# A spectral-mixing and gated-MLP kernel: separate PSUM banks for the inverse transform and the MLP sums, the MLP one pass behind, a fourth bank for its first product and six staging buffers

## The chip, the cores and the metric

The kernel runs on one core of a Trainium2 chip. The metric is the device time of one execution in microseconds. A ratio is the mean time of one kernel's runs over the mean of the other's in the same rounds, so it is not quite the ratio of the medians quoted beside it.

## The reference

```python
batch, seq, dim = 8, 3008, 256          # x: (8, 3008, 256) float32
X = np.fft.rfft(x, axis=1)
y = np.fft.irfft(X * (filt_r + 1j*filt_i)[None], n=seq, axis=1)
t = y.reshape(24064, 256)
h = t @ w_in                            # 256 -> 2048
g = h * (1 / (1 + np.exp(-beta * h)))
out = g @ w_out                         # 2048 -> 256
```

## The kernel before

The first half (to about 618 us) makes cosine and sine tables and does the forward transform and the filter, and passes its result through DRAM. The second half works in 24 passes: three column blocks (512, 512 and 481 columns) of eight batches. Because the transform is real, one pass gives two blocks of tokens, "lo" and "hi". The first product of the MLP is called hps, its sigmoid sig, its gated value gT; the code and the prediction call the MLP "MoE". PSUM, to which TensorE writes its products, is used in banks of 128x512 float32; copying a sum from there to a staging buffer (ostage) is called an eviction.

```python
tc.tile_pool(name="inv_psum", bufs=1, space=PSUM) as ipsum,     # ps0..ps3: four banks
tc.tile_pool(name="moe_psum", bufs=3, space=PSUM) as mpsum,     # hps: three banks
...
for bb in range(B):
    ps = [ipsum.tile([P, 512], F32, tag=f"ps{q}") for q in range(4)]
    psA, psB = ps[0:2], ps[2:4]
    # 24 matmuls with cos into psA; ACT copies psA -> a_sb; 24 with sin into psB
    # DVE: yT_lo = a_sb + psB ; yT_hi = reversed(a_sb - psB)           (4 operations)
    for yT, tbase, jmin, jmax in (lo, hi):
        for fb in range(16):
            hps = mpsum.tile([P, 512], F32, tag="hps")
            # 2 matmuls: hps = w_in[:, fb].T @ yT
            nc.scalar.activation(sig, hps, ACT.Sigmoid, scale=beta)
            nc.vector.tensor_tensor(gT, hps, sig, ALU.mult)
            for tb in range(4):                          # sums in the SAME four banks ps[tb]
                nc.tensor.matmul(ps[tb][:, :256], lhsT=gT[:, tb], rhs=wout_sb[:, fb], ...)
        for tb in range(4):
            ost = mpool.tile([P, 256], F32, tag="ostage")    # three buffers
            nc.scalar.activation(ost, ps[tb][:, :256], ACT.Copy)
            nc.sync.dma_start(out[...], ost[...])
# ... (cut)
```

The program is written in a framework whose scheduler fixes the order of each engine's instructions when the kernel is built. The order therefore stays fixed on the chip.

Of the kernel before, what the change touches and what calls it, by code (L numbers as in the profile page):

```python
# [10 lines left out]
P = 128  # L11

ACT = mybir.ActivationFunctionType
ALU = mybir.AluOpType
F32 = mybir.dt.float32
BF16 = mybir.dt.bfloat16
# [5 lines left out]
def _cdiv(a, b):  # L22
    return (a + b - 1) // b


def _rev_free(ap: AP, count: int) -> AP:
    assert len(ap.shape) == 2 and ap.shape[1] >= count
    base_step = ap.ap[1][0]
    return AP(ap.tensor, ap.offset + (count - 1) * base_step, [ap.ap[0], [-base_step, count]])
# [3 lines left out]
def kernel(  # L33
# [10 lines left out]
    nc = tc.nc  # L44

    B, S, D = x.shape
# [17 lines left out]
    NDC = D // P  # L64
    NFB = FF // P
# [27 lines left out]
    beta_sb = consts.tile([P, NFB], F32, name="beta_sb", tag="beta_sb")  # L93
# [13 lines left out]
    with (  # L107
# [54 lines left out]
        for mm in range(NMH):  # L162
            m0 = mm * P
            pm = min(P, HB - m0)
            j0 = 1 if mm == 0 else 0
            j1 = pm - 1 if (m0 + pm - 1 == KSP) else pm
# [28 lines left out]
        for kb in range(NKB):  # L195
# [5 lines left out]
            for cb in range(NCBF):  # L201
                c0 = cb * CB
                xr_ps = fpsum.tile([P, CB], F32, name="xr_ps", tag="xr_ps")
                xi_ps = fpsum.tile([P, CB], F32, name="xi_ps", tag="xi_ps")
                for mm in range(NMH):
# [4 lines left out]
                        lhsT=cos_tab[:pm, mm, :Kb],  # L210
                        rhs=xe_sb[:pm, mm, c0 : c0 + CB],
                        start=(mm == 0),
                        stop=(mm == NMH - 1),
                    )
                for mm in range(NMH):
# [4 lines left out]
                        lhsT=sin_tab[:pm, mm, :Kb],  # L220
                        rhs=xo_sb[:pm, mm, c0 : c0 + CB],
                        start=(mm == 0),
                        stop=(mm == NMH - 1),
# [43 lines left out]
    with (  # L267
# [3 lines left out]
        tc.tile_pool(name="inv_misc", bufs=2) as imisc,  # L271
        tc.tile_pool(name="moe_sb", bufs=3) as mpool,
        tc.tile_pool(name="inv_psum", bufs=1, space=bass.MemoryType.PSUM) as ipsum,
        tc.tile_pool(name="moe_psum", bufs=3, space=bass.MemoryType.PSUM) as mpsum,
    ):
        def load_inv_tables(icb):
            n0i = icb * 512
            cols = min(512, NMH * P - n0i)
            ct = itab.tile([P, NKB, 512], BF16, name="cos_ti", tag="cos_ti")
            st = itab.tile([P, NKB, 512], BF16, name="sin_ti", tag="sin_ti")  # L280
            nc.sync.dma_start(ct[:, :, :cols], tcos_dram[icb * P : (icb + 1) * P, :, :cols])
            nc.scalar.dma_start(st[:, :, :cols], tsin_dram[icb * P : (icb + 1) * P, :, :cols])
            return ct, st
# [31 lines left out]
        win_sb = wpool.tile([P, NDC, FF], BF16, name="win_sb", tag="win_sb")  # L315
        wout_sb = wpool.tile([P, NFB, D], BF16, name="wout_sb", tag="wout_sb")
        with tc.tile_pool(name="wstage", bufs=1) as wstage:
# [5 lines left out]
            for fb0 in range(0, NFB, WOB):  # L323
# [7 lines left out]
                )  # L331
                nc.vector.tensor_copy(wout_sb[:, fb0 : fb0 + nfb, :], wout_st[:, :nfb, :])

        for ncb in range(NNI):
            n0 = ncb * 512
            Nn = min(512, HB - n0)
            cos_ti, sin_ti = tabs_cur
            if ncb + 1 < NNI:
                tabs_cur = load_inv_tables(ncb + 1)

            hi_jmin = 1 if (n0 <= KSP < n0 + Nn) else 0
            hi_jmax = Nn - 1 if n0 == 0 else Nn

            for bb in range(B):
                ps = []
                for q in range(2 * NDC):
                    pt = ipsum.tile([P, 512], F32, name=f"ps{q}", tag=f"ps{q}")
                    ps.append(pt)
                psA = ps[0:NDC]
                psB = ps[NDC : 2 * NDC]  # L350
                for kk in range(NKB):
                    Kk = min(P, NF - kk * P)
                    for dc in range(NDC):
                        col0 = bb * D + dc * P
                        nc.tensor.matmul(  # L355
                            psA[dc][:, :Nn],
                            lhsT=yr_grps[kk // KKG][:Kk, kk % KKG, col0 : col0 + P],
                            rhs=cos_ti[:Kk, kk, :Nn],
                            start=(kk == 0),
                            stop=(kk == NKB - 1),  # L360
                        )
                a_sb = []
                for dc in range(NDC):
                    at = imisc.tile([P, 512], F32, name=f"a_sb{dc}", tag=f"a_sb{dc}")
                    nc.scalar.activation(at[:, :Nn], psA[dc][:, :Nn], ACT.Copy)  # L365
                    a_sb.append(at)
                for kk in range(NKB):
                    Kk = min(P, NF - kk * P)
                    for dc in range(NDC):
                        col0 = bb * D + dc * P  # L370
                        nc.tensor.matmul(  # L371
                            psB[dc][:, :Nn],
                            lhsT=yi_grps[kk // KKG][:Kk, kk % KKG, col0 : col0 + P],
                            rhs=sin_ti[:Kk, kk, :Nn],
                            start=(kk == 0),
                            stop=(kk == NKB - 1),
                        )
                yT_lo = imisc.tile([P, NDC, 512], BF16, name="yT_lo", tag="yT_lo")
                yT_hi = imisc.tile([P, NDC, 512], BF16, name="yT_hi", tag="yT_hi")
                for dc in range(NDC):  # L380
                    nc.vector.tensor_tensor(  # L381
                        yT_lo[:, dc, :Nn], a_sb[dc][:, :Nn], psB[dc][:, :Nn], ALU.add
                    )
                for dc in range(NDC):
                    nc.vector.tensor_tensor(
                        yT_hi[:, dc, :Nn],
                        _rev_free(a_sb[dc][:, :Nn], Nn),
                        _rev_free(psB[dc][:, :Nn], Nn),
                        ALU.subtract,
                    )  # L390

                nchunk = _cdiv(Nn, P)
                blocks = [
                    (yT_lo, bb * S + n0, 0, Nn),
                    (yT_hi, bb * S + (S - n0 - Nn + 1), hi_jmin, hi_jmax),
                ]
                for yT, tbase, jmin, jmax in blocks:
                    for fb in range(NFB):
                        hps = mpsum.tile([P, 512], F32, name="hps", tag="hps")
                        for dc in range(NDC):  # L400
                            nc.tensor.matmul(  # L401
                                hps[:, :Nn],
                                lhsT=win_sb[:, dc, fb * P : (fb + 1) * P],
                                rhs=yT[:, dc, :Nn],
                                start=(dc == 0),
                                stop=(dc == NDC - 1),
                            )
                        sig = mpool.tile([P, 512], F32, name="sig", tag="sig")
                        nc.scalar.activation(  # L409
                            sig[:, :Nn],  # L410
                            hps[:, :Nn],
                            ACT.Sigmoid,
                            scale=beta_sb[:, fb : fb + 1],
                        )
                        gT = mpool.tile([P, 512], BF16, name="gT", tag="gT")
                        nc.vector.tensor_tensor(gT[:, :Nn], hps[:, :Nn], sig[:, :Nn], ALU.mult)  # L416
                        for tb in range(nchunk):
                            tw = min(P, Nn - tb * P)
                            nc.tensor.matmul(  # L419
                                ps[tb][:tw, :D],  # L420
                                lhsT=gT[:, tb * P : tb * P + tw],
                                rhs=wout_sb[:, fb, :],
                                start=(fb == 0),
                                stop=(fb == NFB - 1),
                            )
                    for tb in range(nchunk):
                        tw = min(P, Nn - tb * P)
                        j0 = max(tb * P, jmin)
                        j1 = min(tb * P + tw, jmax)
                        if j1 <= j0:  # L430
                            continue
                        ost = mpool.tile([P, D], F32, name="ostage", tag="ostage")
                        nc.scalar.activation(ost[:tw], ps[tb][:tw, :D], ACT.Copy)  # L433
                        nc.sync.dma_start(
                            out[tbase + j0 : tbase + j1, :],
                            ost[j0 - tb * P : j1 - tb * P],
                        )


# [28 lines left out]
```

## Time and profile before

| | before |
|---|---|
| time, median (lowest to highest) | 1737.94 us (1735.37 to 1740.11), 12 runs |
| first MLP matmul starts | 618.0 us |
| period of a 512-column pass | 45.74 us, of which TensorE needs 38.3 |
| period of a 481-column pass | 47.85 us, of which TensorE needs 36.8 |
| start of the last evictions to the end of the span | 14.8 us |

The rows of the timeline below read: start, duration, engine and line, operation, output and inputs, shape, count, and in brackets the idle time ahead and who ended it. PE is TensorE (PEld its weight loads), ACT is ScalarE, DVE is VectorE. These are lines of the kernel before that the prediction does not show. First, the shares of the engines in the chain of work that ended last.

```profile
PE 48%; DVE 17%; DMA 15%; ACT 10%; SPq 4%; issue 4%; another core or an unknown queue 2%; ACTq 0%; DVEq 0%
```

```profile
1719.46 0.94 ACT L433 ACTIVATE ostage<-ps 128x256 f32<-128x256 f32 x3 [1.07 <-PE ps L419]
...
1727.17 0.38 ACT L433 ACTIVATE ostage<-ps 97x256 f32<-97x256 f32 x1 [6.78 <-DMA out_dram<-ostage]
```

At the very end the fourth eviction waits 6.78 us for a staging buffer. The view of busy time by stretch shows one pass: its columns are length, busy time (and count) of each engine, granted TensorE clock (1.00 is full speed), DMA share and GB/s.

```profile
core 0: us, PE busy (x) PEld busy (x) DVE busy (x) ACT busy (x) POOL busy (x), PEclk, DMA share, GB/s
...
653.39:699.13 45.74, 41.17 (x236) 21.52 (x241) 23.64 (x36) 24.40 (x43) 0.00 (x0) 1.00 0.07 24
```

TensorE is shown busy 41.2 of 45.7 us, ACT and DVE only half of it.

### The profile page before, as it was taken

The numbers are of one execution on the slowest core, as the hardware profiler recorded it, in microseconds if no ns is written. First come the engines' busy times: TensorE is split into PE (matmuls) and PEld (weight loads), VectorE is DVE, ScalarE is ACT, GpSimd is POOL, SyncE is SP. The second block draws the span as 40 slices with busy tenths as digits, with TensorE's granted clock in tenths as the row PEclk, the third lists the DMA queues.
The fourth block names the chain that finished last, engine by engine and source line by source line (L and its number), as shares of the span: only waits on it lengthen the run. The fifth ranks groups of instructions, "written<-read, shape, count | busy, mean of one in ns | idle before, by whom it ended". The sixth has DMA issues, their size and how long they took to land.

```text
span 1734.2 us, 18868 instructions
## 1 busy us (share of the span) xinstructions
PE 1302.2 (75%) x7100; PEld 665.6 (38%) x7200; DVE 926.4 (53%) x1332; ACT 681.0 (39%) x1322; POOL 4.2 (0%) x19
## 2 busy tenths in 40 slices
PE   0032259999980278898988888999888988888886
PEld 0010024444440034444444444444444544444443
DVE  6044469999980054555554555554555544444444
ACT  1000103333210055555555555555555554444444
POOL 0000000000000000000000000000000000000000
PEclk9965579999995689999999999999999999999998
DMA  4178312212257200000002000000000000000000
GB/s 148 60 248 295 126 55 97 95 70 86 88 193 296 93 22 25 25 25 23 18 22 98 25 25 25 25 25 25 25 25 25 15 21 23 22 14 23 23 24 23
DMA packets 89058, 113.64 MB, mean 66 GB/s; under 512 B 7497, under 2 KB 81923, under 8 KB 87943
## 3 DMA queue, kind: packets, MB, share of 16 engines
q1 hardware_dynamic: 56757, 67.39, 11.6%
q10 hardware_dynamic: 32209, 45.05, 7.5%
q8 instruction: 56, 0.92, 0.2%
q14 instruction: 36, 0.29, 0.1%
HBM read 66.00 MB, written 58.72 MB: 72 GB/s over the span
## 4 chain that ended last, share of the span: by engine, by line
PE 48%; DVE 17%; DMA 15%; ACT 10%; SPq 4%; issue 4%; another core or an unknown queue 2%; ACTq 0%; DVEq 0%
PE ps L419 17%; PE hps L401 11%; DVE gT L416 8%; ACT sig L409 7%; PE ps L371 7%; DMA xb<-xrev_dram 6%; PE ps L355 5%; PE xr_ps L208 4%; DMA out_dram<-ostage 3%; PE xi_ps L218 3%; SPq L169 3%; DMA yr_dram<-yr_stage 2%; ACT ostage L433 2%; DMA yrg<-yr_dram 2%
## 5 line engine op out<-in xcount | busy, mean ns | idle before, releaser
L409 ACT ACTIVATE sig<-hps,beta_sb 128x512 f32<-128x512 f32 (+1 forms) x768 | 498.3, 680 | 383.1 <-PE hps L401 382.8
L416 DVE TENSOR_TENSOR gT<-hps,sig 128x512 bf16<-128x512 f32 (+1 forms) x768 | 500.4, 678 | 263.0 <-ACT sig L409 233.5
L419 PE MATMUL ps<-wout_sb,gT 128*128 128x256 bf16 (+1 forms) x3072 | 470.3, 274 | 85.3 <-DVE gT L416 80.6
L419 PEld LDWEIGHTS <-gT 128*128 128x128 bf16 (+1 forms) x3072 | 262.2, 100 | 357.6 <-DVE gT L416 309.4
L208 PE MATMUL xr_ps<-xe_sb,cos_tab 128*128 128x512 bf16 (+2 forms) x563 | 153.3, 406 | 160.8 <-DVE xe_sb L189 157.5
L381 DVE TENSOR_TENSOR yT_lo<-a_sb,ps 128x512 bf16<-128x512 f32 (+1 forms) x48 | 30.3, 674 | 376.6 <-PE ps L371 376.6
L401 PE MATMUL hps<-yT_lo,win_sb 128*128 128x512 bf16 (+1 forms) x741 | 217.0, 376 | 16.1 <-DVE yT_lo L381 14.8
L401 PE MATMUL hps<-yT_hi,win_sb 128*128 128x512 bf16 (+1 forms) x736 | 225.1, 375 | 1.2
L355 PE MATMUL ps<-cos_ti,yrg 128*128 128x512 bf16 (+3 forms) x565 | 128.8, 381 | 85.5 <-DMA cos_ti<-tcos_dram 46.0
L401 PEld LDWEIGHTS <-win_sb 128*128 128x128 bf16 x1536 | 150.3, 98 | 74.2 <-issue 23.3
L371 PE MATMUL ps<-sin_ti,yig 128*128 128x512 bf16 (+3 forms) x571 | 137.7, 397 | 23.7 <-ACT ostage L433 17.6
L218 PE MATMUL xi_ps<-xo_sb,sin_tab 128*128 128x512 bf16 (+2 forms) x564 | 142.8, 392 | 7.5 <-DVE xo_sb L190 6.9
L208 PEld LDWEIGHTS <-cos_tab 128*128 128x128 bf16 (+1 forms) x576 | 57.3, 104 | 225.3 <-issue 178.6
L355 PEld LDWEIGHTS <-yrg 128*128 128x128 bf16 (+1 forms) x576 | 56.5, 99 | 152.1 <-issue 56.8
L433 ACT ACTIVATE ostage<-ps 128x256 f32<-128x256 f32 x192 | 63.0, 387 | 101.6 <-DMA out_dram<-ostage 75.3
L144 ACT ACTIVATE sstg<-trp 128x128 bf16<-128x128 bf16 x144 | 39.7, 276 | 157.4 <-PE trp L143 144.3
L189 DVE TENSOR_TENSOR xe_sb<-xa,xb 128x2048 bf16<-128x2048 f32 (+1 forms) x12 | 27.5, 2289 | 130.5 <-DMA xb<-xrev_dram 126.4
L371 PEld LDWEIGHTS <-yig 128*128 128x128 bf16 (+1 forms) x576 | 59.0, 102 | 98.5 <-issue 39.5
L365 ACT ACTIVATE a_sb<-ps 128x512 f32<-128x512 f32 (+1 forms) x48 | 25.6, 587 | 168.2 <-PE ps L355 168.2
L105 ACT ACTIVATE cos_tab<-ctmp 128x1536 bf16<-128x1536 f32 x12 | 17.8, 1484 | 179.0 <-DVE ctmp L104 92.4
L218 PEld LDWEIGHTS <-sin_tab 128*128 128x128 bf16 (+1 forms) x576 | 57.9, 102 | 77.4 <-issue 18.8
L144 ACT ACTIVATE cstg<-trp 128x128 bf16<-128x128 bf16 x144 | 39.3, 273 | 44.4 <-PE trp L143 43.3
(45 smaller groups left out, 523.1 us busy)
## 6 DMA issues: line engine op xcount, KB each, us to landing
out_dram<-ostage SPq DMA_DIRECT2D x160, 128.0 KB
xa<-in_x_dram SPq DMA_DIRECT2D x6, 1024.0 KB
yr_dram<-yr_stage SPq DMA_DIRECT2D x11, 512.0 KB
yi_dram<-yi_stage ACTq DMA_DIRECT2D x11, 512.0 KB
xrev_dram<-in_x_dram ACTq DMA_DIRECT2D x5, 1024.0 KB
xrev_dram<-in_x_dram SPq DMA_DIRECT2D x5, 1024.0 KB
xb<-xrev_dram ACTq DMA_DIRECT2D x5, 1024.0 KB
xa<-in_x_dram ACTq DMA_DIRECT2D x5, 1024.0 KB
```

The lines of the kernel that those rows point to most:

```text
L144: nc.scalar.activation(stg[:, mm * P : (mm + 1) * P], trp[:], ACT.Copy)
L169: eng.dma_start(xrev_dram[:, m0 + j0 : m0 + j1, :], AP(x.tensor, x.offset + (S - m0 - j0) * D, [[S * D, B], [-D, j1 - j0], [1, D]],),)
L208: nc.tensor.matmul(xr_ps[:Kb], lhsT=cos_tab[:pm, mm, :Kb], rhs=xe_sb[:pm, mm, c0 : c0 + CB], start=(mm == 0), stop=(mm == NMH - 1),)
L218: nc.tensor.matmul(xi_ps[:Kb], lhsT=sin_tab[:pm, mm, :Kb], rhs=xo_sb[:pm, mm, c0 : c0 + CB], start=(mm == 0), stop=(mm == NMH - 1),)
L355: nc.tensor.matmul(psA[dc][:, :Nn], lhsT=yr_grps[kk // KKG][:Kk, kk % KKG, col0 : col0 + P], rhs=cos_ti[:Kk, kk, :Nn], start=(kk == 0), st ...
L371: nc.tensor.matmul(psB[dc][:, :Nn], lhsT=yi_grps[kk // KKG][:Kk, kk % KKG, col0 : col0 + P], rhs=sin_ti[:Kk, kk, :Nn], start=(kk == 0), st ...
L381: nc.vector.tensor_tensor(yT_lo[:, dc, :Nn], a_sb[dc][:, :Nn], psB[dc][:, :Nn], ALU.add)
L401: nc.tensor.matmul(hps[:, :Nn], lhsT=win_sb[:, dc, fb * P : (fb + 1) * P], rhs=yT[:, dc, :Nn], start=(dc == 0), stop=(dc == NDC - 1),)
L409: nc.scalar.activation(sig[:, :Nn], hps[:, :Nn], ACT.Sigmoid, scale=beta_sb[:, fb : fb + 1],)
L416: nc.vector.tensor_tensor(gT[:, :Nn], hps[:, :Nn], sig[:, :Nn], ALU.mult)
L419: nc.tensor.matmul(ps[tb][:tw, :D], lhsT=gT[:, tb * P : tb * P + tw], rhs=wout_sb[:, fb, :], start=(fb == 0), stop=(fb == NFB - 1),)
L433: nc.scalar.activation(ost[:tw], ps[tb][:tw, :D], ACT.Copy)
```

## The change

The intent is to let the inverse transform of the next pass run while the MLP of the last one waits for its gate, and to give the buffers that the waits hang on more room. Shortened diff:

```diff
-        tc.tile_pool(name="moe_psum", bufs=3, space=PSUM) as mpsum,
+        tc.tile_pool(name="moe_psum", bufs=4, space=PSUM) as mpsum,
+        tc.tile_pool(name="ops_psum", bufs=1, space=PSUM) as opsum,
+        def run_moe(yT, tbase, jmin, jmax, Nn):
+            ...
+                for q in range(_cdiv(nchunk, 2)):        # two sums share one bank
+                    ot = opsum.tile([P, 2, D], F32, name=f"oacc{q}", tag=f"oacc{q}")
+                    accs += [ot[:, 0, :], ot[:, 1, :]]
+            ...                                          # hps, sig, gT as before
+                            start=(fb == 0 and tb % 2 == 0),
+                    ost = mpool.tile([P, D], F32, name="ostage", tag="ostage", bufs=6)
             for bb in range(B):
-                ps = [...four banks...]; psA = ps[0:NDC]; psB = ps[NDC:]
+                psA = [ipsum.tile([P, 512], F32, name=f"psA{q}", tag=f"ps{q}") for q in range(NDC)]    # NDC is 2
                 ...
+                psB = [ipsum.tile([P, 512], F32, name=f"psB{q}", tag=f"ps{q}") for q in range(NDC)]
                 ...
-                for yT, tbase, jmin, jmax in blocks: ...  # MLP of this pass
+                if pending is not None: run_moe(... of the pass before ..., lo); run_moe(..., hi)
+                pending = (yT_lo, yT_hi, ...)
+        run_moe(... last pass ...)
```

## The prediction

> **What bounds the kernel now.** I read the page first, for the engines and the chain that ended last.
>
> ```profile
> PE 1302.2 (75%) x7100; PEld 665.6 (38%) x7200; DVE 926.4 (53%) x1332; ACT 681.0 (39%) x1322; POOL 4.2 (0%) x19
> ...
> PE ps L419 17%; PE hps L401 11%; DVE gT L416 8%; ACT sig L409 7%; PE ps L371 7%; DMA xb<-xrev_dram 6%; PE ps L355 5%; PE xr_ps L208 4%; DMA out_dram<-ostage 3%; PE xi_ps L218 3%; SPq L169 3%; DMA yr_dram<-yr_stage 2%; ACT ostage L433 2%; DMA yrg<-yr_dram 2%
> ```
>
> The chain alternates between TensorE and the ACT/DVE pair of the second half (inverse transform plus MoE), which runs from 618 us to the end. The groups of instructions say who makes whom wait there.
>
> ```profile
> L409 ACT ACTIVATE sig<-hps,beta_sb 128x512 f32<-128x512 f32 (+1 forms) x768 | 498.3, 680 | 383.1 <-PE hps L401 382.8
> L416 DVE TENSOR_TENSOR gT<-hps,sig 128x512 bf16<-128x512 f32 (+1 forms) x768 | 500.4, 678 | 263.0 <-ACT sig L409 233.5
> L419 PE MATMUL ps<-wout_sb,gT 128*128 128x256 bf16 (+1 forms) x3072 | 470.3, 274 | 85.3 <-DVE gT L416 80.6
> ...
> L381 DVE TENSOR_TENSOR yT_lo<-a_sb,ps 128x512 bf16<-128x512 f32 (+1 forms) x48 | 30.3, 674 | 376.6 <-PE ps L371 376.6
> ```
>
> ACT and DVE are each half idle, waiting for TensorE; TensorE waits for gT. It is a latency loop, with no saturated engine. Then the timeline of TensorE for one pass (one column block, one batch; 24 passes).
>
> ```profile
> 653.39 5.34 PE L355 MATMUL ps<-cos_ti,yrg 128*128 128x512 bf16 x23
> 658.57 5.35 PE L371 MATMUL ps<-sin_ti,yig 128*128 128x512 bf16 x24
> 664.55 1.46 PE L401 MATMUL hps<-yT_lo,win_sb 128*128 128x512 bf16 x6 [0.63 <-DVE yT_lo L381]
> 667.08 0.61 PE L419 MATMUL ps<-wout_sb,gT 128*128 128x256 bf16 x4 [1.08 <-DVE gT L416]
> 667.53 0.38 PE L401 MATMUL hps<-yT_lo,win_sb 128*128 128x512 bf16 x1
> 667.75 0.60 PE L419 MATMUL ps<-wout_sb,gT 128*128 128x256 bf16 x4
> 668.18 0.38 PE L401 MATMUL hps<-yT_lo,win_sb 128*128 128x512 bf16 x1
> ```
>
> Starts matter here, as matmul ends are modelled. 24 inverse matmuls take 658.57-653.39 = 5.18 us, 0.216 each; a 512-column hps matmul 0.218 (667.53 to 667.75), four 256-column ones 0.436. Needed per pass: 48 x 0.216 + 64 x 0.218 + 128 x 0.109 = 38.3 us. The next pass starts at 699.13, 45.7 us later; 15 passes from 653.39 to 1340.51 average 45.8. So TensorE loses 7.5 us a pass:
> - about 0.8 us from the end of the inverse (663.75) to the first hps, while DVE makes yT;
> - 1.2 us from the sixth hps (665.86) to the first ps, while the sig/gT pipe fills;
> - about 1.2 us where the low half turns to the high half (gaps of 0.23, 0.57 and some short ones near 684-687) and 1.2 us at the end (0.64, 0.26 and the change to the inverse);
> - about 3 us over the steady part, where eight groups from 667.75 to 675.61 take 7.86 us and need 6.98.
>
> The last eight passes, with 481 columns, need less work and take longer: (1671.74-1384.64)/6 = 47.85 us. Waits and timeline of one:
>
> ```profile
> ACT ostage L433 <- DMA out_dram<-ostage: 6.8, 1, 6.8
> ...
> PE ps L371 <- ACT ostage L433: 2.5, 1, 2.5
> ```
>
> ```profile
> 1437.80 0.37 PE L371 MATMUL ps<-sin_ti,yig 128*128 128x481 bf16 x1
> 1440.63 4.63 PE L371 MATMUL ps<-sin_ti,yig 128*128 128x481 bf16 x22 [2.46 <-ACT ostage L433]
> ```
>
> The fourth eviction waits for one of three staging buffers, whose store takes 7 us, and the second inverse product waits for that bank. At 1679.58 the same stall is followed by 23 matmuls taking 6.11 us, where 24 took 5.04: weight loads come 0.40 us apart instead of 0.20. Together some 3.8 us (47.85 against 44.1 for the first 481-column pass, 1340.51 to 1384.64, that has no such stall).
>
> **What the Trainium skill says.** "DMA: Bandwidth & Descriptors", section "Why a DMA increments its semaphore by 16 and not by 1": a copy uses the largest number of engines up to 16 that divides its slowest dimension; its example of 127 partitions gets one engine. 97 is prime too. The trace agrees: ACT waits 6.8 to 7.1 us behind a 127-row store, but 1.3 us where the same buffer's store has 128 rows. "TensorE: Matmul & The Clock Gate", section "The HAM clock gate": after an idle window the array runs at half clock for a few us; the seven slow steps after 1679.58 agree, though the idle was only 2.8 us. "PSUM — Partial Sum Buffer", "The four PSUM rules": a first matmul clears the accumulate bits of its whole 2 KiB bank, so two groups in one bank may use the flag only on the first one issued; the change does that. No run here shows it yet.
>
> **The change part by part.** No matmul, activation or vector instruction is added or removed. Three things move.
> 1. The inverse of pass i now has its own two banks (psA, then psB in the same two), the MoE sums have two banks of two halves each, hps has four banks instead of three: 8 banks in place of 7. MoE runs one pass behind the inverse.
> 2. Staging buffers for stores go from 3 to 6.
> 3. Because allocations move, the first halves of both weights are loaded during the forward half instead of at its end.
>
> I read the changed kernel's instruction order from its build (the order is static, so it counts). TensorE does, per pass: 37 of the 48 inverse matmuls in a block around the change of passes (psA's end, three hps, all 24 of psB), 6 after the first MoE step, a few at other turns. So the scheduler does not fill the steady gaps with inverse work; it fills the turns.
>
> Stalls left per 512-column pass, by walking that order with durations from the trace: hps issued to usable gT is 0.21 + 0.72 + 0.75 = 1.68 us (1036.16 to 1037.85, ACT at 1036.37, DVE at 1037.09).
> - Steady part: five-step cycle, with 1, 1, 2, 4, 2 hps between steps. Step D's gT is ready at 0.65+1.68 = 2.33 and reached at 2.18: 0.15 lost; one more step of the five loses 0.15. 0.3 per 5 steps, 32 steps: 1.9; with the same method the old four-step cycle gives 0.37, measured 0.36 to 0.52, so I take 2.2.
> - psB waits for two a_sb copies; three hps (0.65) cover: 0.1.
> - psA of the next pass waits for the four yT operations after psB (2.1 us); one step and seven hps cover 1.96: 0.1, and about 0.3 in the following steps as DVE catches up.
> - Low-to-high turn: the bank's evictions (two of 0.3 each, behind four hps worth 0.87) 0.3; last two steps, with one and two inverse matmuls in them: 0.3.
>
> Sum 3.3, a pass 38.3+3.3 = 41.6; I take 41.7, a gain of 4.1. A 481-column pass needs 36.8 (48 x 0.203 + 64 x 0.205 + 128 x 0.109): 40.2, a gain of 7.6, of which 3.8 from the staging buffers.
>
> Sum of the time: the first MoE starts at 618, some 3 us earlier by (3): 615. Then 15 x 41.7 = 625.5; 8 x 40.2 = 321.6 and 0.9 for the MoE of 512 columns in the first of them; the last MoE alone 29.5; ramps 2.5. Last matmul at 1595. Then the tail: in the old kernel 14.6 us from the last matmul (1719.6) to the end, as the last 97-row store waits for a staging buffer until the 127-row store has landed. With six buffers it is issued at once but shares that store's one DMA engine, so I take off half of the 6.8 us wait: 11.2. Span 1606; timed runs are 3 us above the span (1737.2 against 1734.2): 1609 us.
>
> **The rivals.**
> (a) *Full fill*: the inverse and the fourth hps bank remove all stalls: 24 passes at the needed time, about 1530 us. Against it: the order keeps the inverse in blocks, and the steady cycle still runs one latency deep.
> (b) *The wait moves*: with two banks instead of four, psB waits for the copies of psA and the next psA for yT, and hi waits for the evictions of lo. If each cost the 1 us or so that turns cost now, a pass takes 44 us: about 1665. For it: each bank now has a user just ahead. Against: three hps, seven hps, four hps were placed over just these waits.
> (c) *Only the staging buffers pay*: 8 x 3.8 + 3.4 = 34 us, so 1703. It would need the lag to give nothing, against 2 us of fill at every pass start that have work in front of them now.
> (d) *Forward half*: the moved 1 MB weight loads collide with the x loads before 230 us, which set the start there; up to 8 us either way.
> (e) *Clock*: TensorE at 92% could be throttled. The granted clock was 1.00 from 653 to 1066 us at 90% and 0.98 from 330 to 430 at 96%, so no.
>
> **Range and chances.** The stalls left could be half as large (-35 us) or 1 us a pass larger (+24), the forward half +-6, the hand walk some more: 1580 to 1645. Even rival (c) is 2% off the old time, so faster by over 2% gets 0.97, within 2% 0.025, slower 0.005.
>
> **What would show it.** In the profile after: pass period 41 to 42.5 us (first column blocks) and about 40 at 481 columns; no ACT wait for stores over 1 us; the waits of the first hps for yT and of L371 for ostage gone; waits for gT cut by more than half, not to zero; new small waits of psB on the copies and of psA on yT, under 0.3 us each. A period above 43.5 with long psA or psB waits is rival (b); below 39.5 is (a). I would be wrong if the start of the first MoE moved by over 8 us, or if evictions of the shared banks stop TensorE for over 1 us a turn.

## More of the kernel before

Next, the end of the load wait at the middle of the kernel; then the last evictions.

```profile
615.67 1.04 PE L355 MATMUL ps<-cos_ti,yrg 97*128 97x512 bf16 x2 [31.85 <-DMA yrg<-yr_dram]
...
617.97 1.87 PE L401 MATMUL hps<-yT_lo,win_sb 128*128 128x512 bf16 x4 [0.41 <-DVE yT_lo L381]
```

## The result, and the profile after

The changed kernel takes 1585.42 us (1583.92 to 1587.02, 8 runs), a ratio of 0.9124 with a 95% interval of 0.9115 to 0.9133. That lies in the predicted range of 1580 to 1645, 24 us below the predicted 1609. Its page says for the engines and for the chain that ended last:

```profile
PE 1261.2 (80%) x7099; PEld 666.1 (42%) x7200; DVE 923.5 (58%) x1332; ACT 675.9 (43%) x1322; POOL 4.2 (0%) x19
...
PE 68%; DMA 12%; DVE 10%; SPq 4%; another core or an unknown queue 2%; ACT 1%; issue 1%; ACTq 0%; DVEq 0%
```

TensorE now carries 68% of the chain, where it had 48%, and ACT 1% where it had 10%. The groups, in the form of the prediction's (busy, mean ns, then idle time of the engine ahead and who ended most of it):

```profile
L357 ACT ACTIVATE sig<-hps,beta_sb 128x512 f32<-128x512 f32 (+1 forms) x768 | 497.3, 683 | 311.1 <-PE hps L349 288.6
L367 PE MATMUL oacc<-wout_sb,gT 128*128 128x256 bf16 (+1 forms) x3072 | 462.4, 274 | 3.9 <-DVE gT L364 2.6
...
L432 DVE TENSOR_TENSOR yT_lo<-a_sb,psB 128x512 bf16<-128x512 f32 (+1 forms) x48 | 30.4, 674 | 192.0 <-PE psB L422 192.0
```

The idle time of TensorE ahead of the second product fell from 85.3 to 3.9 us. A pass, by stretch, in the columns shown above:

```profile
714.34:754.31 39.97, 39.71 (x237) 21.63 (x241) 23.57 (x36) 24.19 (x43) 0.00 (x0) 1.00 0.08 27
```

The period is 39.97 us (predicted 41.7), and 38.42 at 481 columns (predicted 40.2). TensorE looks fully busy, but the modelled ends hide small gaps, so we read starts. The turn from one pass to the next, in TensorE's timeline:

```profile
674.38 5.38 PE L422 MATMUL psB<-sin_ti,yig 128*128 128x512 bf16 x24
679.60 0.60 PE L367 MATMUL oacc<-wout_sb,gT 128*128 128x256 bf16 x4
680.03 1.67 PE L349 MATMUL hps<-yT_lo,win_sb 128*128 128x512 bf16 x7
681.54 1.46 PE L405 MATMUL psA<-cos_ti,yrg 128*128 128x512 bf16 x5
682.84 0.60 PE L367 MATMUL oacc<-wout_sb,gT 128*128 128x256 bf16 x4
```

Nothing is lost here: 24 matmuls in 5.22 us, four small ones in 0.43, seven in 1.51, and then 1.30 us to the next row, which is six of 0.216 (one record is missing from the trace). The waits for yT and for the copies that the prediction feared are zero. The steady part:

```profile
687.56 0.59 PE L349 MATMUL hps<-yT_lo,win_sb 128*128 128x512 bf16 x2
688.14 0.61 PE L367 MATMUL oacc<-wout_sb,gT 128*128 128x256 bf16 x4
...
690.11 0.38 PE L349 MATMUL hps<-yT_lo,win_sb 128*128 128x512 bf16 x1
690.47 0.61 PE L367 MATMUL oacc<-wout_sb,gT 128*128 128x256 bf16 x4
```

Two hps matmuls need 0.43 us and the next start comes after 0.58; one needs 0.22 and the next start comes after 0.36. So 0.15 us is lost twice per five steps, without any idle time in the record. In the pass from 714.34 there are ten such losses, about 1.5 us, and one of 0.16 us at 736.5, where the sums of hi take over the bank of lo: that is the 1.67 us of 39.97 - 38.3.

The first pass went the other way:

```profile
619.38 1.03 PE L405 MATMUL psA<-cos_ti,yrg 97*128 97x512 bf16 x2 [31.74 <-DMA yrg<-yr_dram]
620.68 7.11 PE L422 MATMUL psB<-sin_ti,yig 128*128 128x512 bf16 x24 [0.26 <-ACT a_sb L415]
628.41 1.46 PE L349 MATMUL hps<-yT_lo,win_sb 128*128 128x512 bf16 x5 [0.62 <-DVE yT_lo L432]
```

The loads end 3.7 us later than before, and now all 24 psB matmuls follow them (7.1 us, at a mean granted clock of 0.75), because psB shares its banks with psA; before, 22 of them had run between the loads. The first MLP matmul starts at 628.4 instead of 618.0 us.

Last, the tail: the evictions of the changed kernel, and the GB/s of its last 18 us in 40 slices of 0.45 us.

```profile
1569.10 1.20 ACT L382 ACTIVATE ostage<-oacc 128x256 f32<-128x256 f32 x4 [1.18 <-PE oacc L367]
```

```profile
GB/s 18 0 0 0 0 0 0 0 0 0 0 0 7 20 16 27 152 273 128 68 23 25 25 23 25 23 25 18 9 25 23 25 23 25 25 23 25 11 0 0
```

All four evictions run at once, and still the end comes 13.6 us after their start, against 14.8. The two 128-row stores are the burst up to 273 GB/s; the rest of the 127-row store and then the 97-row store go one after the other at 23 to 25 GB/s.

### The profile page after: what moved, and what is told of

Its sections match the earlier page's. It is cut to its first block, busy times and chain, and to the rows that moved or that the text cites. A ratio compares the mean times of both kernels' runs of the same rounds, so it can differ in the third digit from the quotient of the medians. Undisturbed runs are those within 1.5% of the kernel's fastest.

```text
span 1582.7 us, 18763 instructions
## 1 busy us (share of the span) xinstructions
PE 1261.2 (80%) x7099; PEld 666.1 (42%) x7200; DVE 923.5 (58%) x1332; ACT 675.9 (43%) x1322; POOL 4.2 (0%) x19
## 4 chain that ended last, share of the span: by engine, by line
PE 68%; DMA 12%; DVE 10%; SPq 4%; another core or an unknown queue 2%; ACT 1%; issue 1%; ACTq 0%; DVEq 0%
PE oacc L367 24%; PE hps L349 20%; PE psB L422 8%; PE psA L405 8%; DMA xb<-xrev_dram 6%; PE xr_ps L208 4%; PE xi_ps L218 4%; SPq L169 4%; DMA yi_dram<-yi_stage 2%; DMA yrg<-yr_dram 2%; DMA xrev_dram<-in_x_dram 1%; PE trp L143 1%; DVE xo_sb L190 1%; DVE yi_stage L260 1%
## 5 line engine op out<-in xcount | busy, mean ns | idle before, releaser
L357 ACT ACTIVATE sig<-hps,beta_sb 128x512 f32<-128x512 f32 (+1 forms) x768 | 497.3, 683 | 311.1 <-PE hps L349 288.6
L367 PE MATMUL oacc<-wout_sb,gT 128*128 128x256 bf16 (+1 forms) x3072 | 462.4, 274 | 3.9 <-DVE gT L364 2.6
L405 PE MATMUL psA<-cos_ti,yrg 128*128 128x512 bf16 (+3 forms) x569 | 144.6, 385 | 93.6 <-DMA cos_ti<-tcos_dram 47.3
L349 PE MATMUL hps<-yT_hi,win_sb 128*128 128x512 bf16 (+1 forms) x737 | 215.3, 375 | 1.1
L349 PE MATMUL hps<-yT_lo,win_sb 128*128 128x512 bf16 (+1 forms) x737 | 209.0, 375 | 1.6 <-DVE yT_lo L432 0.6
L432 DVE TENSOR_TENSOR yT_lo<-a_sb,psB 128x512 bf16<-128x512 f32 (+1 forms) x48 | 30.4, 674 | 192.0 <-PE psB L422 192.0
L422 PE MATMUL psB<-sin_ti,yig 128*128 128x512 bf16 (+3 forms) x569 | 128.3, 378 | 0.7 <-ACT a_sb L415 0.3
L415 ACT ACTIVATE a_sb<-psA 128x512 f32<-128x512 f32 (+1 forms) x48 | 25.8, 587 | 159.8 <-PE psA L405 159.8
L143 PE MATMUL trp<-ident,cos_tab 128*128 128x128 bf16 x144 | 32.7, 227 | 54.3 <-ACT cstg L144 30.8
L144 ACT ACTIVATE cstg<-trp 128x128 bf16<-128x128 bf16 x144 | 39.3, 273 | 72.8 <-PE trp L143 41.7
```

Source lines behind the costliest of these rows:

```text
L143: nc.tensor.transpose(trp[:], tab[:, mm, :], ident[:])
L144: nc.scalar.activation(stg[:, mm * P : (mm + 1) * P], trp[:], ACT.Copy)
L349: nc.tensor.matmul(hps[:, :wsub], lhsT=win_sb[:, dc, fb * P : (fb + 1) * P], rhs=yT[:, dc, c0 : c0 + wsub], start=(dc == 0), stop=(dc == N ...
L357: nc.scalar.activation(sig[:, :wsub], hps[:, :wsub], ACT.Sigmoid, scale=beta_sb[:, fb : fb + 1],)
L367: nc.tensor.matmul(accs[tb][:tw, :D], lhsT=gT[:, tb * P : tb * P + tw], rhs=wout_sb[:, fb, :], start=(fb == 0 and tb % 2 == 0), stop=(fb = ...
L405: nc.tensor.matmul(psA[dc][:, :Nn], lhsT=yr_grps[kk // KKG][:Kk, kk % KKG, col0 : col0 + P], rhs=cos_ti[:Kk, kk, :Nn], start=(kk == 0), st ...
```

## The experiments

Every kernel below gave a correct result; those with the banks of the changed kernel hold two sums in one bank with the flag on the first matmul alone, so that part of the prediction is borne out. "Period" is the distance between the starts of psB (in kernels without psB, of the sine product) in neighbouring passes.

| kernel | time, us | ratio to before | period 512 | period 481 |
|---|---|---|---|---|
| before | 1738 | 1 | 45.74 | 47.85 (mean) |
| before, six staging buffers | 1689.8 | 0.9723 | 44.74 | 43.18 |
| before, four hps banks | 1693.9 | 0.9739 | 43.99 | 45.6 (mean) |
| before, split stores | 1702.3 | 0.9795 | 45.75 | 44.14 |
| changed, no lag | 1617.5 | 0.9303 | 41.38 | 39.90 |
| changed, three staging buffers | 1613.0 | 0.9283 | 40.16 | 40.86 |
| changed, three hps banks | 1603.2 | 0.9234 | 40.43 | 39.45 (mean) |
| changed, inverse between the steps | 1594.1 | 0.9176 | 40.46 | 39.03 |
| changed | 1585.4 | 0.9124 | 39.97 | 38.42 |
| changed, first psB in other banks | 1581.3 | 0.9101 | 39.99 | 38.44 |
| changed, as a stream | 1554.4 | 0.8948 | 38.85 | 37.33 |
| stream, first psB, split stores | 1539.6 | 0.8864 | 38.85 | 37.33 |
| changed, middle rows split | 1528.5 | 0.8801 | 39.99 | 38.44 |
| stream, first psB, stores, middle rows and x split | 1414.0 | 0.8142 | 38.85 | 37.33 |

My theory at the start: TensorE's need is the floor, the latency loop hps, sig, gT sets the steady loss, and the turns and the store stall are the rest, filled by lag, banks and buffers. The rivals: the fourth bank or the banks alone give the gain; or the stall of the stores is a matter of buffer count only; or filling gaps with any independent work removes them.

**Six staging buffers alone.**

```diff
-   ost = mpool.tile([P, D], F32, name="ostage", tag="ostage")
+   ost = mpool.tile([P, D], F32, name="ostage", tag="ostage", bufs=6)
```

> The kernel before with six staging buffers for stores in place of three, nothing else. My theory: the only thing that goes is the stall of the 481-column passes (2.5 us of wait plus 1.3 us of slow clock, in 7 passes, 27 us) and a little of the tail (1 to 3 us), so about 1709 us; the 481-column period falls from 47.85 to about 44.1 us and the 512-column period stays at 45.8. Rival (the store stall was hidden elsewhere or the slow clock is not its consequence): 1720 or more, with slow weight loads still there.

It gave 48 us, not 29. The 481-column stall is gone as expected (43.18), but the 512-column period fell by 1.0 us too (15 us of the 48), which I had not expected. ACT's timeline at the turn from lo to hi shows most of the reason; first the kernel before:

```profile
682.49 0.93 ACT L433 ACTIVATE ostage<-ps 128x256 f32<-128x256 f32 x3
...
685.18 0.37 ACT L433 ACTIVATE ostage<-ps 128x256 f32<-128x256 f32 x1
```

Then the same with six buffers:

```profile
730.82 1.21 ACT L433 ACTIVATE ostage<-ps 128x256 f32<-128x256 f32 x4
```

With three buffers the scheduler put three activations ahead of the fourth eviction, and the hi half's first sum in that bank starts at 685.60, just after it. With six it evicts four in a row. By starts TensorE loses about 0.7 us less at this turn; the other 0.3 us lie at the end of the pass, where the order differs too. A buffer count thus changed the order of the build, besides the waits on the chip.

**Four hps banks alone.** `bufs=3` becomes `bufs=4` in the kernel before.

> The kernel before with four hps banks in place of three. My theory: the steady loss falls from 3 us to about 1.6 us a pass (0.3 us per five steps), the waits at the turns stay, so the 512-column period falls from 45.8 to about 44.3 and the time to about 1703. Rival (a bank more does nothing, as the loop is one latency deep either way, and all gain is from running the MoE a pass behind): 1735 or more.

The period fell by 1.75 us (44.3 expected, 43.99 measured) and the time to 1693.9 us (1703 expected), so the bank does help by itself and the rival of no effect falls.

**Split stores, three buffers.**

```diff
-   nc.sync.dma_start(out[tbase+j0 : tbase+j1], ost[j0-tb*P : j1-tb*P])
+   ja = j0 + (j1 - j0)//16*16
+   for s0, s1 in ((j0, ja), (ja, j1)):
+       if s1 > s0: nc.sync.dma_start(out[tbase+s0 : tbase+s1], ost[s0-tb*P : s1-tb*P])
```

> The kernel before, three staging buffers, but each store of 97 or 127 rows is issued as a part with a multiple of 16 rows and a rest. Theory of the one-engine store: the wait of the fourth eviction falls from 6.8 us to under 2 us, no TensorE stall in the 481-column passes (period about 44.1), and the tail of 14.6 us falls to about 7: about 1703 us. Rival (the number of buffers is what matters, whatever the store's speed): within 5 us of 1738.

This met its numbers (1702.3 us, period 44.14, tail of 5.4 us after the start of the evictions). ACT's wait in a 481-column pass and the last eviction:

```profile
ACT ostage L433 <- DMA out_dram<-ostage: 1.5, 1, 1.5
```

```profile
1697.48 0.38 ACT L433 ACTIVATE ostage<-ps 97x256 f32<-97x256 f32 x1 [1.50 <-DMA out_dram<-ostage]
```

So the stall came from the speed of the 127-row store. More buffers hide it, splitting the awkward stores removes it, and the 512-column period does not move (45.75), which sets this part apart from the order effect above.

**The changed kernel without the lag.** run_moe is called for the present pass right after its inverse.

> The changed kernel with its banks and buffers, but the MoE of each pass run right after its inverse, not one pass behind. My theory: the yT wait (0.8 us) and the fill of the sig/gT pipe (1.2 us) come back at each pass, so the 512-column period is about 42 us (40.0 after, 45.8 before), 481 columns 40.4, and the time about 1628. Rival (the banks alone give the gain, the lag nothing): within 8 us of 1585. Rival (the lag is nearly all): above 1680.

The lag is worth 1.41 us a pass, not 2.0. The wait for yT is back:

```profile
797.13 1.89 PE L349 MATMUL hps<-yT_lo,win_sb 128*128 128x512 bf16 x8 [0.63 <-DVE yT_lo L431]
```

By starts it costs 0.8 us. The other part is a wait that the expectation did not name: psB now waits for the copies of psA, as no hps of the pass before lie between them.

```profile
791.15 5.34 PE L421 MATMUL psB<-sin_ti,yig 128*128 128x512 bf16 x23 [0.47 <-ACT a_sb L414]
```

By starts that is 0.63 us, and the two waits make up the 1.41. The fill of the pipe, 1.2 us in the kernel before, costs little here: eight hps matmuls and four of the next psA lie in front of the first sum. The separate banks alone let the next inverse start while this MLP still runs. Against six buffers and four hps banks added up (45.74 - 1.00 - 1.75 = 42.99) this kernel is 1.6 us a pass better. That would be what the separate banks give if the two effects added; no run here has both without the separate banks, so it is not shown.

**The changed kernel with three staging buffers.**

> The changed kernel with three staging buffers, the old number. If the buffers are worth what they were alone (512-column period 45.74 to 44.74, 481-column 47.85 to 43.18): 41.0 and about 43, total about 1640. My theory, that the inverse matmuls now cover part of the eviction wait: 512-column period within 0.5 us of 39.97, 481-column about 42 (the wait of 7 us is longer than the cover of some 3 us), about 1615.

Close to my numbers: 40.16 and 40.86. The waits of one 481-column pass:

```profile
ACT ostage L382 <- DMA out_dram<-ostage: 5.0, 1, 5.0
...
PE oacc L367 <- DVE gT L364: 2.0, 1, 2.0
```

ACT still waits 5 us for the one-engine store, and as its sigs queue behind that, TensorE loses 2.0 us to a late gT and no longer to a late copy. The buffers are worth 28 us here, 48 us in the kernel before.

**The changed kernel with three hps banks.**

> The changed kernel with three hps banks. Its order now places one inverse matmul in every fourth step of the steady part, where a step loses 0.37 us with three banks; so my theory is that the filled matmul (0.22) takes most of that loss: 512-column period 39.5 to 40.4, time within 15 us of 1585. Rival (the fourth bank is worth the 1.75 us a pass that it was alone): period 41.7, about 1625.

The period is 40.43, a hair above my window, and the time 18 us above the changed kernel's, not within 15: a near miss. The bank is worth 0.46 us per 512-column pass here, 1.75 alone. The steady losses are no larger than with four banks, as the scheduler had placed inverse matmuls in the gaps; what is new is that psA waits for yT in nearly every pass, with five hps ahead of it where the changed kernel has seven:

```profile
762.81 1.46 PE L405 MATMUL psA<-cos_ti,yrg 128*128 128x512 bf16 x6 [0.24 <-DVE yT_hi L436]
```

By starts this is 0.40 us, nearly the whole 0.46. The bank and the lag overlap in what they give, so their single gains must not be added.

**psB of the first pass in the banks of the sums.**

```diff
+   if ncb == 0 and bb == 0:
+       psB = [opsum.tile([P, 2, D], F32, tag=f"oacc{q}").rearrange("p a d -> p (a d)") for q in range(NDC)]
+   else:
        psB = [ipsum.tile([P, 512], F32, tag=f"ps{q}") for q in range(NDC)]
```

> The changed kernel, but in the first pass alone psB has the two banks of the MoE sums, so that the second inverse product can run while the loads come in, as in the kernel before. My theory: the first MoE matmul moves from 628.4 to about 622 us and the time from 1585 to about 1579; nothing else changes. Rival (the later start is all from the loads): within 2 us of 1585.

4 us less, 6 expected: psB of the third pass starts at 670.86 instead of 674.38. My check, the first MLP matmul, was badly chosen: it comes later here (630.2), as the first product of the second pass's inverse now runs ahead of it, and as the last load ends 2.7 us later in this profile (622.06).

**The inverse written between the MLP steps.** Before each step, two matmuls of the next inverse are emitted.

> The changed kernel with the inverse of the next pass written between the MoE steps, two matmuls a step. The built order runs hps only two steps ahead: from hps issued to its use there are 1.53 us of matmuls. Theory of the latency loop of 1.68 us: about 0.15 us lost in each of some 24 steps, so 41 to 43 us a 512-column pass and 1600 to 1650 us, slower although every gap is filled with inverse work. Rival (filling gaps with independent work removes the stalls): period 38.5, about 1550.

It is slower than the changed kernel, as the latency theory said and the rival did not, but by 0.5 us a pass only: period 40.46, just under my window, and 1594 us, just under 1600. A loss in its timeline:

```profile
802.93 0.38 PE L398 MATMUL psA<-cos_ti,yrg 128*128 128x512 bf16 x1
803.30 0.61 PE L369 MATMUL oacc<-wout_sb,gT 128*128 128x256 bf16 x4
```

0.37 us from one matmul of 0.22 to the next group: 0.15 lost. By starts, twelve steps of the pass from 805.82 lose 0.12 to 0.16 us each and the others little or nothing, where I had counted 24 losses. Work in the gaps is no help if the distance from hps to its use shrinks.

**One stream, hps three steps ahead.** The MLP steps of all passes are one sequence: for each step, the sums of step s, then one unit of the next inverse (two matmuls, or one yT operation), then hps, sig and gT of step s+3. There are five staging buffers and four for gT, for room.

```diff
+   for s in range(NPASS * 32):
+       emit_o(s)                    # four sums of step s
+       next(inverse_of_next_pass, None)
+       emit_h(s + 3)                # two hps matmuls, sig, gT
```

> The changed kernel's banks and lag, but written as one stream of MoE steps with hps always three steps ahead of its use and two inverse matmuls after each step (five staging buffers, four gT buffers). Between hps and its use lie over 2.1 us of matmuls, more than the 1.68 us loop. Theory of the latency loop: almost no steady loss, 512-column period 38.3 to 38.7 (needed: 38.3), 481-column 36.8 to 37.2, time about 1552. Rival (the 1.7 us a pass that the changed kernel still loses are the turns: evictions, copies, yT): period stays near 39.5 to 40, time 1575 or more.

1554.4 us, 1552 expected; the periods are 38.85 and 37.33, each 0.1 to 0.2 above my window. The steps now follow almost without a loss, 0.43 us per group:

```profile
803.38 0.59 PE L408 MATMUL hps<-yT_hi,win_sb 128*128 128x512 bf16 x2
803.81 0.60 PE L452 MATMUL oacc<-wout_sb,gT 128*128 128x256 bf16 x4
```

So what the changed kernel still lost was the latency loop, and distance plus filling removes two thirds of it (0.55 us a pass are left of 1.67). What the distance, the filling and the extra gT buffer each give was not tested apart.

**Three further versions.** The stream with the first psB in other banks and with split stores:

> The stream, with psB of the first pass in the banks of the MoE sums and with stores split into a multiple of 16 rows and a rest. Theory: 4 us less from the first pass as measured before, and 5 to 6 us less in the tail (13.6 us after the last matmul becomes about 8): about 10 us below the stream. Rival (the tail is a fixed cost of the last store): 4 us below.

It is 15 us below the stream. The tail after the start of the evictions is 4.9 instead of 13.7 us, so the tail is mostly the one-engine stores. The first MLP matmul comes 6.5 us earlier.

The changed kernel with the 97-row writes and reads between the halves split into 96 and 1:

> The changed kernel, but the 97-row writes and reads of the transformed blocks between the two halves are each split into 96 rows and 1. If the wait of 31 us before the first inverse ends is the work of one DMA engine, the last inverse matmul of the first pass moves from 619 to about 580 us and the time from 1585 to about 1548. Rival (the wait is for the total of the loads): within 8 us of 1585.

57 us less, 37 expected: the last inverse load lands by 563.3 instead of 619.4 us.

```profile
563.28 1.03 PE L411 MATMUL psA<-cos_ti,yrg 97*128 97x512 bf16 x2 [1.76 <-DMA yrg<-yr_dram]
```

I had counted the reads that come last; the 97-row writes that they wait for are slow too: the last reads are issued at 537 and 538 instead of 563 and 566 us, and even the first inverse matmul moved from 563.8 to 536.8.

And the stream with all of these, and the loads of x split too:

> Stream, first pass in own banks, stores split, and all loads and writes of 97 or 127 partitions split to a multiple of 16 and a rest, those of x too. If the effects add: stream -33, first pass and tail -10, middle -37, and two stretches at about 24 GB/s in the first 225 us that shrink by some 50 us: about 1455 us.

1414.0 us, 0.8142 of the kernel before and the fastest here; 1455 was expected. The first MLP matmul starts at 497.3 us, against 622.8 in the stream without the splits of the middle and of x. If the middle gives its 57 us here too, the x splits give some 69 of these 125.5, where 50 had been expected; they were not run alone.

## Why the prediction was right or wrong

- *What bounds the kernel*: right. No engine was full, and the kernels that shorten or cover the latency loop, the turns and the store stall moved the period as the table shows.
- *The store stall*: right in cause and size (3.8 us a pass; by the split stores 47.85 to 44.14). It missed that three buffers also made the built order worse by 1.0 us in every pass, mostly at the lo/hi turn; I had put this turn down to the banks. The slow matmuls that it saw after one stall follow five of the seven stalls of the kernel before, so its 3.8 is a mean.
- *Stalls left per pass*, 3.3 us in the prediction, was the mis-sized term, with 1.67 measured. The steady mechanism held to the digit (0.15 us, twice per five steps), but ten losses in a pass make 1.5, not the 2.2 I took for 32 steps. The turns, put at 1.1 us, cost about 0.2 beyond these ten: psB's wait for the copies and psA's for yT (0.1 each, and 0.3 after) came out at zero, the low-to-high turn (0.3) at 0.16, and the last two steps (0.3) are two of the ten. This is 1.7 us in 15 passes and 1.8 in eight, 40 us too slow.
- *First MLP matmul 3 us earlier*: wrong in sign. It came 10.4 us later, and over 8 us was the prediction's own sign of being wrong. 3.7 of this are the first half: the last xe operation (the sum that prepares x for the forward transform) ends its wait at 233.4 instead of 230.6 us, and the one-engine reads end later. The record shows that this goes with the staging buffers. In all four kernels with three of them the weight loads start at 499 us or later and this wait ends at 230.6 to 232.0; in the nine with five or six (the one with x split left out) the first two start at 175 to 225 us and it ends at 233.2 to 235.1. Six buffers in the kernel before, with no other edit, do this too, and three in the changed kernel undo it. So the moved loads go with a start about 3 us later, where the prediction had them save 3, which is its rival (d); what exactly they collide with was not tested. The rest is psB of the first pass behind psA in the same banks, which the prediction had not allowed for; moving it to other banks gave 4 us back.
- *The tail*: 13.6 us instead of 11.2, and 14.8 before. The two slow stores do go one after the other, as the prediction said of a shared engine; I gave the six buffers half of the 6.8 us wait and they got 1.1 us of it, since the two stores together take as long as before.
- *The sum*: 40 us too slow in the passes, 13 too fast at the start, 2 at the tail. The errors partly cancel in the 24 us by which the prediction missed. With the error of the passes alone the time would have been 1569 us, below the range of 1580 to 1645, and both periods lie below the 41 to 42.5 and about 40 that it named: that the time fell into the range was partly luck.
- *Rivals*: full fill (1530) did not happen, for the reason given: the order keeps the inverse in blocks. "The wait moves" did not happen in the changed kernel, but its waits appear as soon as the cover goes: psB's for the copies without the lag (0.63 us), psA's for yT with three hps banks (0.40 us). "Only the staging buffers pay" fell: they are worth 28 us in the changed kernel, which gained 153 in all. "Forward half" came true, at about 3 us. The clock stayed at 1.00 from 640 to 1060 us, with TensorE shown busy 99% of the time.

## What to carry to other kernels

Read a loss from starts, not from idle time, when matmul ends are modelled, and find the distance in work between a product and its use: here 1.53 us of work did not cover a loop of 1.68 us through the other engines, over 2.1 us did, and filling helped only where it kept that distance. Buffer counts change the built order and the placing of loads as well as the waits, so try each alone and do not add single gains. Beside adding buffers for a slow transfer, look at its row count: splitting off a multiple of 16 rows took 36 us from the kernel before without a buffer (three more buffers took 48), and 57 us in the middle of the changed one.

## What the Trainium skill lacked or had wrong

- "DMA: Bandwidth & Descriptors", "Why a DMA increments its semaphore by 16 and not by 1": its rule of the largest divisor fits the copies of 97 and 127 rows here, but the section does not say what such a copy costs. The page's section "Specifications" does, with about 27 GiB/s (29 GB/s) per engine; the slow stores of the tail ran at 23 to 25 GB/s and the 97-row reads of the middle at 26 to 27. Splitting such stores took 36 us off the kernel before, and splitting the middle's 97-row copies 57 us off the changed one.
- "TensorE: Matmul & The Clock Gate", "Back-to-back issue gap": it states about 131 ns per matmul for N=512 in a real stream with weight loads. Here the dense stretches of 512 columns that were read, with a weight load for each matmul, ran at 216 to 218 ns a matmul, which is the page's isolated figure (about 216).
- The same page, "The HAM clock gate": it names an idle window of about 3.4 us before the clock halves. In the kernel before, TensorE stood idle for 2.44 to 2.80 us (2.6 to 3.0 by starts) seven times; after five of these, seven to nine matmuls came 0.40 us apart instead of 0.20 (granted clock 0.55 from 1679.58 to 1682.50), after two none did. A shorter idle time was thus enough here, and its length alone did not decide: 2.46 us before 1440.63 brought no slow matmul, 2.45 us before 1392.34 did.
- "Perfetto Trace Analysis", "Identifying the Most-Contended Engine": it warns that matmul busy time is a bad measure. In this profile it goes so far that 39.71 of 39.97 us read as busy while starts show 1.67 us lost; for TensorE the page does not say to compare starts.
